# Full-row dummies and tap broadcast, and filter block 1 transposed beside the rows of y, in a fused SSM and GEGLU kernel

## The chip, the cores and the metric

The kernel runs on one core of a Trainium2 chip. The metric is the device time of one execution in microseconds (us), taken as the median of several runs. A core has five engines with a queue of instructions each: TensorE (PE, matmuls, its weight loads shown as PEld), VectorE (DVE), ScalarE (ACT), GpSimd (POOL) and SyncE (SP, which here only issues DMAs). They wait for each other through semaphores. Matmuls write to PSUM; the kernel uses PSUM as four slots of two banks, a slot being 128 partitions of 2 x 512 32-bit words.

## The reference, cut to what matters

Four sublayers act on x of 2048 positions and 576 channels (bf16): an SSM convolution, a gated feed-forward of width 4608, and both once more.

```python
def _A_ref(q, k, v, shift_k, ssm_k, ssm_D):
    for t in range(ks):                       # ks = 4
        k_shift = k_shift + k_pad[:, t:t + S, :] * shift_k[:, ks - 1 - t][None, None, :]
    kv = k_shift * v
    kv_f, kf_f = rfft(pad(kv)), rfft(pad(ssm_k))
    y = irfft(kv_f * kf_f)[:S] + kv * ssm_D
    return q * y
def _B_ref(x, w_gate, w_up, w_down):
    return (_gelu(x @ w_gate) * (x @ w_up)) @ w_down
x = A_q
x = x + _A_ref(_layernorm(x), A_k, A_v, A_shift_k, A_ssm_k, A_ssm_D)
x = x + _B_ref(_layernorm(x), B_w_gate, B_w_up, B_w_down)
...
```

The last two lines are applied a second time with the same weights.

## The kernel before

The 2048 positions are cut into four blocks of 512, and a block into four rows of 128 partitions (row j holds positions 4p + j). The convolution is done by block with transforms of length 512 written as matmuls, so each block of `kv` and of the filter `ssm_k` is transformed by matmuls with a matrix T of sines, multiplied on VectorE and transformed back with V, the transpose of T. The feed-forward of a block runs over 36 tiles of 128 hidden columns in three passes: gate and up matmuls (`gu`, L1008), Gelu on ScalarE, the product on VectorE, then down matmuls (`dn`, L1576). The convolutions of later blocks are woven into these matmuls.

The opening, up to the first gate/up matmuls of block 0, is laid out by a planner (`Plan`): each piece of work is a task with an engine, a cost, tasks it depends on, a priority, and sometimes a PSUM slot (`bank=True`) that comes free when all tasks naming it in `frees` have run. The planner puts the tasks in an order by these costs, and each engine's queue is written in that order. What the steps of the change touch there, in order of time:

- `ones` (L1101, L1110) is a tile of one row, and 16 dummy matmuls (L1137) use it for both operands while the first loads come in.
- `sk1` (L1099) holds the four taps of the shift filter in one row. `tap` (L1187) broadcasts each tap over 128 partitions by a matmul with `ones` (L1191), and ScalarE copies it to `skc` (L1193).
- VectorE multiplies the block's `k` by the taps (L1209), TensorE sums these products in PSUM with an identity or a shifted identity (L1218), and VectorE multiplies the sums by `v` (L1229).
- `turned_h` (L1238) transposes a block of the filter, loaded as `hn`, with TensorE (L1251): two groups of ten transposes, each with a PSUM slot of its own, each copied out by ScalarE for block 0 and by VectorE for block 1 (L1253). Block 1's come last, with the lowest priority; they are next read by the filter's transform woven into the feed-forward (L290).
- Filter block 0 and `kv` block 0 are transformed (L281, L275), multiplied (L316 to L320) and transformed back to y (L1340): rows 0 and 2 as soon as the products come, rows 1 and 3 after them. The four rows of y take the four PSUM slots. A row of y uses 288 of the 512 columns of each bank.
- `busy` (L1366): ten times four dummy matmuls with the identity, into spare columns of the slot of row 1 of y.
- For each row j, in the order 0, 2, 1, 3 of the source: `factor` (L1385, ScalarE, reads y and makes `yh`), `gate` (L1394, VectorE, makes the new x and its sum), `nm` and `nu` (L1399, L1401: the negative mean, twice, scaled in two ways), the copy of y out of PSUM (L1404, ScalarE), `square` (L1411, ScalarE), `root` (L1419, L1420, GpSimd), `norm` (L1427, VectorE, makes `xn`), ten transposes of `xn` (L1439, L1441, TensorE) into a PSUM slot, and the copy to `xnT` (L1446 by VectorE, L1449 by ScalarE).
- `gu_half`: the first two gate/up tiles start with half of the columns, those of rows 0 and 2, as soon as these two are there.

In the order that the planner made, row 2 comes first, then 0, 3 and 1.

Of the kernel before, what the change touches and what calls it, by code (L numbers as in the profile page):

```python
# [10 lines left out]
ACT = mybir.ActivationFunctionType  # L11
# [682 lines left out]
def ssm_geglu_kernel(ctx, tc, A_q, A_k, A_v, A_shift_k, A_ssm_k, A_ssm_D, B_x, B_w_gate, B_w_up,  # L694
# [394 lines left out]
    with tc.manual_schedule():  # L1089
# [6 lines left out]
        with ExitStack() as es:  # L1096
            tmp = es.enter_context(tc.tile_pool(name="s_tmp", bufs=1))
            hp = es.enter_context(tc.tile_pool(name="s_h", bufs=1))
            sk1 = tmp.tile([1, D, conv.KS], BF16, name="sk1")  # L1099
            drow = tmp.tile([1, D], BF16, name="drow")  # L1100
            ones = tmp.tile([1, P], BF16, name="ones")  # L1101

            def load_hn(b):
# [5 lines left out]
                return hn  # L1109
            nc.vector.memset(ones[:], 1.0)  # L1110
            below = tmp.tile([P, P], BF16, name="below")
            for grid in (ident, below):
                nc.gpsimd.memset(grid[:], 0.0)
            nc.sync.dma_start(out=sk1[:].rearrange("p d j -> p (d j)"),
                              in_=A_shift_k.rearrange("d j -> (d j)").unsqueeze(0))
# [19 lines left out]
            ps = bank(3, "ps")  # L1135
            for _ in range(16):
                nc.tensor.matmul(ps[:, 0, 0:P], lhsT=ones[:], rhs=ones[:], start=True, stop=True)  # L1137
# [46 lines left out]
            vneg = add("ACT", 0.9, vnegs, [vsin], prio=-20.0)  # L1184


            def tap(j):  # L1187
                def fill_ps(task):
                    ps = psum(("tap", j), task)
                    for h in range(2):  # L1190
                        nc.tensor.matmul(ps[:, h, 0:HW], lhsT=ones[:], rhs=sk1[:, h * HW:(h + 1) * HW, j], start=True, stop=True)  # L1191
                a = later(lambda me: add("PE", 0.5, me(fill_ps), bank=True, ready=2.9))
                return add("ACT", 0.65, lambda: nc.scalar.copy(out=conv.halves(conv.skc[:, j, :]),  # L1193
                                                               in_=held.pop(("tap", j))[:, :, 0:HW]), [a], lat=0.1, frees=[a])
# [42 lines left out]

            def turned_h(b, dep, ready, prio):  # L1238
                outs = []
                for g in range(RT // 2):  # L1240
                    def fill_ps(task, g=g):
                        if b == 0 and g == 0:
                            hT[0] = lambda i: hT0[:, i, :]
                        elif b == 1:
                            pairs1.append(conv.hrp.tile([P, 2, D], BF16, tag="hr", name="ht"))
                            hT[1] = conv.ht[1] = lambda i: pairs1[i // 2][:, i % 2, :]
                        pt = psum(("h", b, g), task, (P, 2, 1024), BF16)
                        for i in range(2):
                            for db in range(ND):
                                w = min(P, D - db * P)  # L1250
                                nc.tensor.transpose(pt[:, i, db * P:db * P + w], hn[b][0:w, db, 2 * g + i:BS:RT], ident[0:w, 0:w])  # L1251
                    a = later(lambda me: add("PE", 1.05, me(fill_ps), dep, bank=True, ready=ready, prio=prio))
                    outs.append(add("DVE" if b else "ACT", 0.8 if b else 1.12, lambda g=g: (nc.vector.tensor_copy if b else nc.scalar.copy)(out=hT0[:, 2 * g:2 * g + 2, :] if b == 0 else pairs1[g][:], in_=held.pop(("h", b, g))[:, :, 0:D]),  # L1253
                                    [a], lat=0.1, frees=[a], prio=prio))
                return outs

            h0 = {}

            def filter_tile(m, deps):
# [12 lines left out]
                return outs  # L1272
            t0 = turned_h(0, [], HN_AT, 30.0)
            for a in opens:
# [89 lines left out]
            def busy():  # L1364
                for _ in range(4):
                    nc.tensor.matmul(held["y", 1][:, 1, 384:512], lhsT=ident[:], rhs=ident[:], start=True, stop=True)  # L1366
            chain([add("PE", 0.22, busy, [inv[1], inv[3]], frees=[opened[1]], prio=-100.0) for _ in range(10)])


# [11 lines left out]
            for j in (0, 2, 1, 3):  # L1381

                def factor(j=j):
                    held["yh", j] = tmp.tile([P, 2, HW], F32, tag="yh", bufs=2, name="yh")
                    nc.scalar.activation(out=held["yh", j][:], in_=held["y", j][:, :, 0:HW], func=ACT.Identity,  # L1385
                                         scale=g0[j]["rstd"][:, 0:1], bias=1.0)
                fa = add("ACT", 0.65, factor, [inv[j], stat[j]] + pluses[-2:-1], lat=0.1)

                def gate(j=j):
# [8 lines left out]
                    v["nm"] = small.tile([P, 1], F32, tag="l_nm", name="nm")  # L1398
                    nc.vector.tensor_single_scalar(out=v["nm"][:], in_=v["s"][:], scalar=-1.0 / D ** 1.5, op=ALU.mult)  # L1399
                    v["nu"] = small.tile([P, 1], F32, tag="nu", name="nu")  # L1400
                    nc.vector.tensor_single_scalar(out=v["nu"][:], in_=v["s"][:], scalar=-1.0 / D, op=ALU.mult)  # L1401
                gp = add("DVE", 1.1, gate, [fa])
                pluses.append(gp)
                copies[j] = add("ACT", 0.65, lambda j=j: nc.scalar.copy(out=conv.halves(conv.y[0][:, j, :]), in_=held.pop(("y", j))[:, :, 0:HW]),  # L1404
                    [fa], frees=[opened[j]], prio=-10.0)

                def square(j=j):
                    v = vs0[j]
                    v["ss"] = small.tile([P, 1], F32, tag="ss", name="ss")
                    junk = work.tile([P, D], BF16, tag="ga", name="junk")  # L1410
                    nc.scalar.activation(out=junk[:], in_=x_c[0][:, j, :], func=ACT.Square, bias=v["nm"][:, 0:1],  # L1411
                                         scale=1.0 / math.sqrt(D), accum_out=v["ss"][:])
                sq = add("ACT", 0.96, square, [gp], lat=0.1)

                def root(j=j):
                    v = vs0[j]
                    v["rstd"] = small.tile([P, 1], F32, tag="l_rstd", name="rstd")
                    ve = small.tile([P, 1], F32, tag="ve", name="ve")
                    nc.gpsimd.tensor_scalar(out=ve[:], in0=v["ss"][:], scalar1=EPS, scalar2=None, op0=ALU.add)  # L1419
                    nc.gpsimd.tensor_tensor(out=v["rstd"][:], in0=ve[:], in1=neghalf_t[:, 0:1], op=ALU.pow)  # L1420
                rt = add("POOL", 0.85, root, [sq], lat=0.05)

                def norm(j=j):
                    v = vs0[j]
                    xn, entry = xn_tile()
                    held["xn", j], entry[0] = xn, True
                    nc.vector.tensor_scalar(out=xn[:, 0:D], in0=x_c[0][:, j, :], scalar1=v["nu"][:, 0:1],  # L1427
                                            scalar2=v["rstd"][:, 0:1], op0=ALU.add, op1=ALU.mult)
                no = add("DVE", 0.6, norm, [rt])

                def turn_xn(task, j=j):
# [3 lines left out]
                    for b in range(NKC):  # L1435
# [5 lines left out]
                        nc.tensor.transpose(pt[:, b // 8, (b % 8) * P:(b % 8 + 1) * P], held["xn", j][:, c0:c0 + P], ident[:])  # L1441
                tx = later(lambda me: add("PE", 0.55, me(turn_xn), [no], bank=True))
                tok = slice(j * P, (j + 1) * P)
# [10 lines left out]

            t1 = turned_h(1, [loads[1]] + [pA[part, m, 0] for part in range(2) for m in (0, 2)] + H0[3] + K0[3], 0.0, -30.0)
            conv.nhr = 6
# [218 lines left out]
```

## Time and profile before

| what | us |
|---|---|
| median of three runs | 929.02 (928.86 to 929.34) |
| the profiled run's own time | 928.66 |
| its span in the profile | 926.9 |
| TensorE busy | 917.0 |
| first dummy matmul | 1.06 |
| filter block 0 transposed from | 6.61 |
| y transformed back from, to | 31.04, 36.92 |
| first transposes of xn | 41.02 |
| first half gate/up matmul | 44.03 |

The profile is of one execution. A line of the timeline gives the start and the length of a group of like instructions (the length reaches to the end of the last one, which overlaps with what follows), engine, line, operation, the tiles written and read, shape and type, and how many; in square brackets stands the time for which the engine had been idle, and what it was waiting for. The share of the span is written in tenths or per cent; the granted clock of TensorE is a number from 0 to 1.

### The profile page before, as it was taken

To read this page: it belongs to the slowest core of one execution; us is meant where nothing else is said; L and a number is where in the kernel's file an instruction comes from. 1 tells how busy PE (TensorE), PEld (TensorE's weight loads), DVE (VectorE), ACT (ScalarE), POOL (GpSimd) and SP (SyncE) were. 2 spreads that over 40 slices of the span, in tenths; PEclk is the share of its full clock that TensorE was granted. 3 is DMA by queue.
4 is the path that set the end of the run, shared out by engine and by line. 5 is a ranking of instruction groups with operands and counts; after the bars stand their busy time and mean duration, and the time that the engine had idled before them with its cause. 6 is when DMAs were issued, how large, how long until landed. Compare 5 with 4: busy or idle time off the path is not lost.

```text
span 926.9 us, 19167 instructions
## 1 busy us (share of the span) xinstructions
PE 917.0 (99%) x8103; PEld 529.8 (57%) x8103; DVE 579.7 (63%) x1109; ACT 325.7 (35%) x594; POOL 139.9 (15%) x305
## 2 busy tenths in 40 slices
PE   9999999999999999999999999999999999999998
PEld 6746456564664655646646646546556556556555
DVE  7876876777898898768988873553332334433332
ACT  6664525643215136252122223451221224321211
POOL 3314102312014002230112101220000002100000
PEclk9999999999999999999999999999999999999999
DMA  9899997337726901991952820690820730797620
GB/s 238 267 236 239 265 254 139 117 77 218 205 65 153 251 2 21 218 281 36 240 166 76 168 78 27 124 196 15 152 80 1 145 87 14 132 214 162 144 68 27
DMA packets 125307, 129.69 MB, mean 140 GB/s; under 512 B 39714, under 2 KB 117411, under 8 KB 125220
## 3 DMA queue, kind: packets, MB, share of 16 engines
q1 hardware_dynamic: 116018, 92.92, 46.9%
q0 software_dynamic: 9056, 34.95, 11.7%
q8 instruction: 63, 1.03, 0.5%
q10 hardware_dynamic: 146, 0.59, 0.2%
q14 instruction: 24, 0.20, 0.1%
HBM read 108.09 MB, written 11.80 MB: 129 GB/s over the span
## 4 chain that ended last, share of the span: by engine, by line
PE 95%; DVE 2%; ACT 1%; issue 0%; DMA 0%; POOL 0%; ACTq 0%; DVEq 0%; SPq 0%
PE gu L1008 60%; PE dn L1576 28%; PE ps L281 1%; PE cps L290 1%; PE cps L343 1%; PE ps L1218 1%; DVE kc L602 1%; PE cps L301 0%; PE ps L1008 0%; PE ps L1340 0%; PE ps L1251 0%; DVE ab L308 0%; DVE cd L308 0%; ACT eo L303 0%; DMA xnT<-xn 0%
## 5 line engine op out<-in xcount | busy, mean ns | idle before, releaser
L1008 PE MATMUL gu<-xnT,wgu 64*128 64x512 bf16 x5148 | 561.1, 376 | 2.3 <-DVE x_c L1618 1.5
L1008 PEld LDWEIGHTS <-wgu 64*128 64x128 bf16 x5220 | 255.2, 94 | 304.3 <-issue 9.9
L1557 ACT ACTIVATE ga<-gu 128x512 f32<-128x512 f32 x256 | 152.8, 597 | 471.4 <-PE gu L1008 465.3
L1558 DVE TENSOR_TENSOR hT<-ga,gu 128x512 bf16<-128x512 f32 x256 | 175.5, 685 | 204.3 <-ACT ga L1557 203.0
L1576 PE MATMUL dn<-wd,hT 128*128 128x288 bf16 x2304 | 294.1, 286 | 0.0
L1576 PEld LDWEIGHTS <-hT 128*128 128x128 bf16 x2304 | 223.5, 98 | 65.3 <-issue 9.3
L840 POOL TENSOR_SCALAR means<-s 128x1 f32<-128x1 f32 x28 | 11.8, 421 | 237.7 <-DVE x_c L1612 205.3
L1620 DVE TENSOR_TENSOR x_c<-x_c,dn 128x576 f32<-128x576 f32 x32 | 24.1, 752 | 31.0 <-PE dn L1576 30.9
L1618 DVE SCALAR_TENSOR_TENSOR x_c<-dn,means,x_c 128x576 f32<-128x576 f32 x28 | 22.7, 815 | 26.8 <-PE dn L1576 26.7
L856 POOL TENSOR_TENSOR rstd<-ve,neghalf_t 128x1 f32<-128x1 f32 x56 | 35.5, 635 | 4.7
L320 DVE TENSOR_TENSOR prod<-prod 128x576 bf16<-128x576 bf16 x72 | 33.0, 458 | 2.5
L1547 ACT ACTIVATE ga<-gu 128x512 bf16<-128x512 f32 x30 | 17.9, 597 | 44.1 <-PE gu L1008 42.1
L303 ACT ACTIVATE eo<-cps 128x576 f32<-128x576 f32 x32 | 20.4, 650 | 25.0 <-DVE ab L308 9.8
L418 POOL DMA_DIRECT2D kr<-Kd x24 | 13.2, 550 | 87.1 <-DVE prod L319 86.1
L1599 DVE TENSOR_TENSOR xn<-x_c,dn 128x576 bf16<-128x576 f32 x15 | 11.3, 752 | 24.0 <-PE dn L1576 23.9
L422 POOL DMA_DIRECT2D hr<-Hd x36 | 19.4, 540 | 41.2 <-DVE prod L319 38.5
L602 DVE TENSOR_TENSOR kc<-ab,cd 128x288 bf16<-128x288 f32 x64 | 25.6, 450 | 0.0
L1549 DVE TENSOR_TENSOR hT<-ga 128x512 bf16<-128x512 bf16 x31 | 13.1, 421 | 18.5 <-ACT ga L1548 18.5
L840 POOL TENSOR_SCALAR nm<-s 128x1 f32<-128x1 f32 x28 | 8.7, 312 | 99.9 <-DVE x_c L892 99.8
L848 ACT ACTIVATE junk<-x_c,nm 128x576 bf16<-128x576 f32 x28 | 21.5, 767 | 4.9 <-POOL nm L840 4.9
L882 ACT ACTIVATE yh<-y,rstd 128x576 f32<-128x576 bf16 x28 | 21.4, 768 | 2.3 <-POOL rstd L856 2.3
L855 POOL TENSOR_SCALAR ve<-ss 128x1 f32<-128x1 f32 x56 | 15.3, 273 | 42.9 <-ACT junk L848 42.8
(170 smaller groups left out, 607.1 us busy)
## 6 DMA issues: line engine op xcount, KB each, us to landing
wgu<-in_B_w_gate_dram SPq DMA_DIRECT2D x45, 576.0 KB, 6.2
wd<-in_B_w_down_dram SPq DMA_DIRECT2D x30, 864.0 KB, 8.0
wgu<-in_B_w_up_dram SPq DMA_DIRECT2D x45, 512.0 KB, 8.3
hr<-Hd POOLq DMA_DIRECT2D x36, 288.0 KB, 7.9
kr<-Kd POOLq DMA_DIRECT2D x24, 288.0 KB, 6.7
Kd<-kc POOLq DMA_DIRECT2D x12, 288.0 KB, 6.3
k<-in_A_k_dram POOLq DMA_DIRECT2D x3, 1008.0 KB, 11.1
wgu<-in_B_w_up_dram SPq DMA_DIRECT2D x45, 64.0 KB, 8.7
```

The source lines that it names most:

```text
L320: nc.vector.tensor_tensor(out=dst[:, cols], in0=pr[:, 0, cols], in1=pr[:, 1, cols], op=ALU.subtract if part == 0 else ALU.add)
L602: nc.vector.tensor_tensor(out=into[k][:, plane, cols], in0=a, in1=b, op=op)
L840: nc.gpsimd.tensor_scalar(out=v["nm"][:], in0=v["s"][:], scalar1=-1.0 / D, scalar2=None, op0=ALU.mult)
L848: nc.scalar.activation(out=junk[:], in_=get_x(), func=ACT.Square, bias=v["nm"][:, 0:1], accum_out=v["ss"][:])
L856: nc.gpsimd.tensor_tensor(out=v["rstd"][:], in0=ve[:], in1=neghalf_t[:, 0:1], op=ALU.pow)
L882: nc.scalar.activation(out=g["yh"][:], in_=conv.y[c][:, j, :], func=ACT.Identity, scale=g["rstd"][:, 0:1], bias=1.0)
L1008: nc.tensor.matmul(cols(pair[:, s, :]), lhsT=w[r0:r0 + HK, k, gi * P:(gi + 1) * P], rhs=cols(xnT[r0:r0 + HK, blk_of[k], :]), start=(k == 0 ...
L1557: nc.scalar.activation(out=ga[:], in_=pair[:, 0, :], func=ACT.Gelu_apprx_tanh)
L1558: nc.vector.tensor_tensor(out=hT[:, fi, :], in0=ga[:], in1=pair[:, 1, :], op=ALU.mult)
L1576: nc.tensor.matmul(acc[:, h, 0:HW], lhsT=hT[:, fi, j * P:(j + 1) * P], rhs=wd[2 * wb + fi // WT][:, fi % WT, h * HW:(h + 1) * HW], start=( ...
L1618: nc.vector.scalar_tensor_tensor(out=xh, in0=acc[:, :, 0:HW], scalar=m_[:, 0:1], in1=xh, op0=op, op1=ALU.add)
L1620: nc.vector.tensor_tensor(out=xh, in0=xh, in1=acc[:, :, 0:HW], op=ALU.add)
```

## The change

1. `ones` gets 128 rows, and the dummies are 18 instead of 16. `sk1` gets 97 rows: the taps are loaded to the last one, the others are set to zero by VectorE, and the tap broadcast multiplies 97 rows. After the last tap two more dummies (`spare`) write to spare columns of its slot.
2. `turned_h` is split. Block 0's stays as it was. Block 1's (`turned_h1`) takes no PSUM slot: of its two groups the columns from 128 on go into unused columns of the slots of rows 1 and 3 of y, seen as bf16, and the first 128 columns of both groups into the slot of row 0. Four copies by VectorE (two of 2 x 128 columns, two of 2 x 448) take the place of two of 1152 columns. The slots of rows 0, 1 and 3 come free only after these copies too.
3. `busy` is 8 times 4 dummies of 96 columns instead of 10 times 4 of 128, in the slot of row 0.
4. Priorities: the factor of row 1, the squares and roots of rows 0 and 2, and the copies of y. `nu` goes; `nm` takes its scale, and the square and the root are scaled to suit.

In the order of the changed program TensorE has all twenty transposes of block 1 right behind y's rows, then the dummies, and none between the gate/up matmuls. On ScalarE the order of kinds is unchanged; of the last three copies of y, row 3 now comes before 0, and row 1 last. On VectorE the first strip copy stands before the gate of row 1, the copy out of row 3's slot after it and before the norm of row 2, the second strip after the norm of row 3, and the copy out of row 1's slot between the two copies to `xnT`. The queues of GpSimd and SyncE keep their order.

```diff
-            sk1 = tmp.tile([1, D, conv.KS], BF16, name="sk1")
+            SK = 3 * P // 4
+            sk1 = tmp.tile([SK + 1, D, conv.KS], BF16, name="sk1")
-            ones = tmp.tile([1, P], BF16, name="ones")
+            ones = tmp.tile([P, P], BF16, name="ones")
...
+            nc.vector.memset(sk1[0:SK, :, :], 0.0)
...
-            nc.sync.dma_start(out=sk1[:].rearrange("p d j -> p (d j)"),
+            nc.sync.dma_start(out=sk1[SK:SK + 1, :, :].rearrange("p d j -> p (d j)"),
...
-            for _ in range(16):
+            for _ in range(18):
                 nc.tensor.matmul(ps[:, 0, 0:P], lhsT=ones[:], rhs=ones[:], start=True, stop=True)
...
+            def spare(ps):
+                for _ in range(2):
+                    nc.tensor.matmul(ps[:, 1, 3 * P:4 * P], lhsT=ones[:], rhs=ones[:], start=True, stop=True)
...
-                        nc.tensor.matmul(ps[:, h, 0:HW], lhsT=ones[:], rhs=sk1[:, h * HW:(h + 1) * HW, j], start=True, stop=True)
+                        nc.tensor.matmul(ps[:, h, 0:HW], lhsT=ones[0:SK + 1, :], rhs=sk1[:, h * HW:(h + 1) * HW, j], start=True, stop=True)
+                    if j == 0:
+                        spare(ps)
...
+            def turned_h1(dep):
+                W = D - P
+                beside = lambda j: held["y", j].bitcast(BF16)
+                hT[1] = conv.ht[1] = lambda i: pairs1[i // 2][:, i % 2, :]
+                for g, j in ((0, 1), (1, 3)):
+                    def fill_ps(g=g, j=j):
+                        pairs1.append(conv.hrp.tile([P, 2, D], BF16, tag="hr", name="ht"))
+                        for i in range(2):
+                            for db in range(ND):
+                                w = min(P, D - db * P)
+                                out = beside(j)[:, i, 2 * HW + (db - 1) * P:2 * HW + (db - 1) * P + w] if db else \
+                                    beside(0)[:, g, 2 * HW + i * P:2 * HW + (i + 1) * P]
+                                nc.tensor.transpose(out, hn[1][0:w, db, 2 * g + i:BS:RT], ident[0:w, 0:w])
+                    a = add("PE", 1.05, fill_ps, dep + [opened[0], opened[1], opened[3]], prio=-30.0)
+                    add("DVE", 0.2, lambda g=g: nc.vector.tensor_copy(
+                        out=pairs1[g][:, :, 0:P], in_=beside(0)[:, g, 2 * HW:2 * HW + 2 * P].rearrange("p (i d) -> p i d", i=2)),
+                        [a], frees=[opened[0]], prio=-10.0 if g else 10.0)
+                    add("DVE", 0.6, lambda g=g, j=j: nc.vector.tensor_copy(
+                        out=pairs1[g][:, :, P:D], in_=beside(j)[:, :, 2 * HW:2 * HW + W]), [a], frees=[opened[j]], prio=3.0 if g else -30.0)
...
-                    nc.tensor.matmul(held["y", 1][:, 1, 384:512], lhsT=ident[:], rhs=ident[:], start=True, stop=True)
-            chain([add("PE", 0.22, busy, [inv[1], inv[3]], frees=[opened[1]], prio=-100.0) for _ in range(10)])
+                    nc.tensor.matmul(held["y", 0][:, 1, 416:512], lhsT=ident[:], rhs=ident[:, 0:96], start=True, stop=True)
+            chain([add("PE", 0.22, busy, [inv[1], inv[3], opened[0]], frees=[opened[0]], prio=-100.0) for _ in range(8)])
...
-                fa = add("ACT", 0.65, factor, [inv[j], stat[j]] + pluses[-2:-1], lat=0.1)
+                fa = add("ACT", 0.65, factor, [inv[j], stat[j]] + pluses[-2:-1], lat=0.1, prio=15.0 if j == 1 else 0.0)
...
-                    nc.vector.tensor_single_scalar(out=v["nm"][:], in_=v["s"][:], scalar=-1.0 / D ** 1.5, op=ALU.mult)
-                    v["nu"] = small.tile([P, 1], F32, tag="nu", name="nu")
-                    nc.vector.tensor_single_scalar(out=v["nu"][:], in_=v["s"][:], scalar=-1.0 / D, op=ALU.mult)
+                    nc.vector.tensor_single_scalar(out=v["nm"][:], in_=v["s"][:], scalar=-1.0 / D, op=ALU.mult)
...
-                    [fa], frees=[opened[j]], prio=-10.0)
+                    [fa], frees=[opened[j]], prio=-50.0 if j == 1 else -30.0 if j == 0 else -10.0)
...
-                nc.gpsimd.tensor_scalar(out=ve[:], in0=v["ss"][:], scalar1=EPS, scalar2=None, op0=ALU.add)
+                nc.gpsimd.tensor_scalar(out=ve[:], in0=v["ss"][:], scalar1=1.0 / D, scalar2=EPS, op0=ALU.mult, op1=ALU.add)
...
-            t1 = turned_h(1, [loads[1]] + [pA[part, m, 0] for part in range(2) for m in (0, 2)] + H0[3] + K0[3], 0.0, -30.0)
+            turned_h1([loads[1], inv[1], inv[3]])
```

## The prediction

> **What bounds the kernel now.** I read the page first: engines, then the chain of work that ended last.
>
> ```profile
> PE 917.0 (99%) x8103; PEld 529.8 (57%) x8103; DVE 579.7 (63%) x1109; ACT 325.7 (35%) x594; POOL 139.9 (15%) x305
> ...
> PE 95%; DVE 2%; ACT 1%; issue 0%; DMA 0%; POOL 0%; ACTq 0%; DVEq 0%; SPq 0%
> ```
>
> TensorE is busy for 99% of the span. So time can be won in two ways only: PE works faster, or PE is given less to do. The edits all lie before the first gate/up matmuls, so next I read the timeline of PE over the first 50 us.
>
> ```profile
> 1.06 1.88 PE L1137 MATMUL ps<-ones 1*128 1x128 bf16 x16 [1.06 <-DVE pis L1132]
> 3.00 2.20 PE L1191 MATMUL ps<-sk,ones 1*128 1x288 bf16 x8
> 5.48 1.12 PE L1218 MATMUL ps<-kvt,below 128*128 128x288 bf16 x4 [0.28 <-ACT skc L1193]
> 6.61 2.95 PE L1251 MATMUL ps<-ident,hn 128*128 128x128 bf16 x20
> 9.49 1.62 PE L1218 MATMUL ps<-kvt,below 128*128 128x288 bf16 x6
> 10.91 1.32 PE L1218 MATMUL ps<-kvt,ident 128*128 128x288 bf16 x6
> 12.06 0.61 PE L1180 MATMUL ps<-ident,T 128*128 128x128 bf16 x8
> ...
> 13.73 1.88 PE L1218 MATMUL ps<-kvt,ident 128*128 128x288 bf16 x14
> ...
> 36.92 1.04 PE L1251 MATMUL ps<-ident,hn 128*128 128x128 bf16 x10
> 38.13 2.39 PE L1366 MATMUL ps<-ident 128*128 128x128 bf16 x40 [0.18 <-ACT yh L1385]
> 41.02 0.38 PE L1441 MATMUL ps<-ident,xn 128*128 128x128 bf16 x4 [0.49 <-ACT y L1404]
> ...
> 44.03 2.14 PE L1008 MATMUL ps<-xnT,wgu 64*128 64x256 bf16 x36
> 46.10 1.07 PE L1251 MATMUL ps<-ident,hn 128*128 128x128 bf16 x10
> 46.95 1.19 PE L1008 MATMUL ps<-xnT,wgu 64*128 64x256 bf16 x18
> ```
>
> Two things are to be seen. First, the same 128x288 matmul starts every 0.24 us from 9.49 (six in 1.42 us) but every 0.123 us from 13.73 (14 until 15.45); the six from 10.91 take 1.15 us, so the change of rate falls among them, near 11.7 (three at 0.24, then 0.12). PE runs at half rate until then, though the granted clock reads 1.00 in every window. Second, from 5.48 to 30.3 PE is never idle; it is idle again at 30.3 to 31.0, 38.0 to 38.1 and 40.5 to 41.0. At 46.10, with PE in demand, ten transposes of filter block 1 stand on the path: 46.10 to 46.95.
>
> **Head: full-row dummies and taps.** In the old kernel the dummies (L1137) and the tap broadcast (L1191) use one row of the array. They kept PE going from 1.06 to 5.2 at half rate (16 dummies, 0.107 us each) and did not raise it: the first full-row work begins at 5.48, the rate rises near 11.7. The new dummies use 128 rows, the taps 97 (96 of zeros). Two dummies more (0.21 us) fit the wait before 3.00, two spare ones after the last tap the 0.28 us before 5.48: nothing.
>
> If full-row work counts from 1.06, the rate rises 11.7 - 5.48 = 6.2 us after it or sooner, that is by 7.3. The Trainium skill (TensorE: Matmul & The Clock Gate, Part 1: The HAM clock gate) says that PE starts at half clock and is released after one busy window of about 3.4 us that runs freely, not from the kernel's start. By that alone the old kernel would be fast by 7.9 at the latest; the trace says 11.7, so here one-row work did not count; for the new one an estimate from the page is 4.5 to 7.9.
>
> Worth at full rate: the first four matmuls (5.48) end early but the transposes still wait until 6.61 for `hn` (the view of that tile shows 0.7 us of PE waiting for its two transfers). Twenty transposes took 2.88 us (6.61 to 9.49); at full rate ten take 0.85 (46.10 to 46.95) to 1.04 (36.92), so 0.96 each and 0.12 for the second piece of `hn`: 2.04, a gain of 0.84. Twelve accumulating matmuls took 2.57 (9.49 to 12.06), at 0.123 they take 1.47: gain 1.10. Sum 1.94. If the rate rises at 7.3, five transposes go at the old 0.144 instead of 0.096: 0.24 less. I take 1.9.
>
> Can the others follow? VectorE's fourth product ends at 4.53 + 4 x 0.68 = 7.3, before its matmuls; the product with `v` (L1229) then starts at 10.1 instead of 12.02. By the view of DMA issues `v` lands 6.2 us after its issue at 2.23, so at 8.4, and `x_b` for the statistics 7.1 after 2.85, at 9.95, before they are wanted at 12.7. ScalarE's first copy of the transposes moves from 8.15 to 7.85, the second from 9.59 to 8.95; the table load (1.28), `V` copy and negations behind it move 0.7 to 1.2, and it had 0.74 us idle at 16.63; it just keeps up. From 17.4 to 30.4 PE is contiguous, so the gain stays.
> The new memset of 96x1152 words on VectorE has no row; the memset of 128 columns took 0.17, which scales to 1.5 at most, and the smallest took 0.06. I take 1.2, nearer the first. It moves the angle steps from 1.91 to about 2.2 and the products by 0.1 to 0.4; the cover is the wait for `hn`. Without it, 0.4 would be lost.
>
> **Tail: filter block 1.** In the old kernel its second ten transposes run at 46.10, because the first ten hold a bank from 36.92 to the copy at 41.63 and no further bank is free. Now all twenty follow y in unused columns of its banks 0, 1 and 3, and the ten at 46.10 go: from the last half gate/up matmul (44.03 + 36 x 0.0545 = 45.99) to 46.95 is 0.96, and the wait of the next filter matmuls (48.08) for their copy (47.20 + 0.76) goes too, 0.1. Gain 1.06 at most.
>
> What it pushes, in times of the old trace (all minus the head's gain): twenty transposes 36.92 to 38.85. The factor of row 1 (L1385, the second of two at 36.71, begun at 37.35) reads a bank just written, so it stands behind the first ten: 38.05, 0.7 late. Behind it on ScalarE wait the squares, on VectorE the gate of row 1. The old dummies in spare columns of row 1's bank, which began only on "ACT yh L1385", show that waits go by bank, not by column.
>
> ```profile
> 36.71 1.37 ACT L1385 ACTIVATE yh<-ps,rstd 128x576 f32<-128x576 f32 x2
> 37.97 0.77 ACT L1411 ACTIVATE junk<-x_c,nm 128x576 bf16<-128x576 f32 x1
> ...
> 40.35 1.16 ACT L1404 CAST y<-ps 128x576 bf16<-128x576 f32 x2
> 41.94 1.12 ACT L1449 COPY xnT<-ps 128x1152 bf16<-128x1152 bf16 x1 [0.44 <-PE ps L1441]
> ```
>
> - ScalarE: squares at 38.67, 39.43 and 40.27, copies of y 3 and y 0 at 41.05 and 41.57 to 42.2, then xnT at 42.1.
> - VectorE: gate 3 to 38.45; a strip of 256 columns, which needs the sixteenth transpose (38.6); by the 1152-column copy of 0.75 it takes 0.2 (0.06 to 0.75 bound it); gate 1 38.9 to 39.9; 896 columns 0.6, to 40.45; xn of row 2 40.45 to 41.0 (old: 39.46), row 0 to 41.5, row 3 to 42.1, the second strip after y 0's copy to 42.5, row 1 to 43.1. Four times 0.07 for `nu` is saved.
> - PE: the four rows take 0.73 each from 41.05, 41.78, 42.51, 43.25 and end at 44.0; the old ones began at 41.02, held by "ACT y L1404", and ended at 44.03.
>
> So the bank's wait goes, VectorE takes its place, and the half matmuls start as before. The tight spot is the second strip (42.5 against 42.51): late by up to 0.5 if both new copies cost their 0.75, on time otherwise. Tail: 1.06 less 0.5 at worst, gain 0.95 taken. The smaller dummy block (32 x 96 columns for 40 x 128) lies in PE's wait from 39.0 to 41.0: nothing, unless the clock falls (below). From there the orders of all engines are the old ones but for a few products of VectorE that swap places and one pair of down matmuls; PE is the bound, and its waits at 159 to 168, 194 to 198 and 229 to 244 hang on chains that move with it: nothing, give or take 0.3.
>
> **Sum.** 1.9 + 0.95 = 2.85 off the profiled run's 928.66 (span 926.9 and 1.8 around it) gives 925.8. The median shown, 929.02, lies 0.36 above that run, which would give 926.2. I forecast 926.0.
>
> **Rivals.**
> - *The clock rises no sooner* (the edit does not do what it says): zeros and ones for operands, or work this early, do not count. For it: work at 1.06 to 5.2 counted for nothing once. Against: all that differed was its rows. The head then gives 0, the tail 0.95: 929.02 - 0.95 = 928.1.
> - *The tail gives its gain back.* The factor's 0.7 and the new copies go through ScalarE and VectorE to the fourth xn instead of into PE's old wait of 0.49. For it: the second strip has no slack. Only the head is left: 929.02 - 1.9 = 927.1.
> - *Slower: the clock falls before the gate/up matmuls.* Now twenty transposes follow y, then a dummy block shorter by a third (32 x 96 against 40 x 128 columns), then forty transposes. If transposes do not count as work, the clock falls near 41. Against: in the old trace 40.3 to 44.0 had nothing but transposes and a pause and stayed fast (44.03, 36 half matmuls in 2.07). Price: the forty transposes take 2.9 us and would take half as long again (0.144 against 0.096 in the head), 1.5 more, and half rate for the 6.2 us of the head from 44.0 on, 3.1; with both gains kept 929.02 - 2.85 + 4.6 = 930.8. It decides once half rate lasts over 2.7 us into the matmuls (2.85 - 1.5 = 1.35 lost, twice that long).
> The Trainium skill (TensorE: Matmul & The Clock Gate, Part 4: PE-mode transpose) says that transposes do not count as PE-busy in the same way and that the full clock does not engage for them; in this trace transposes from 36.92 on go at full rate, so I give the rival little.
>
> **Chances and range.** Forecast 0.62, clock no sooner 0.15, tail gives back 0.12, slower 0.07, nothing at all 0.04. Measurement tells a change from none beyond 0.2%, 1.86 us, that is below 927.16. Faster: 0.60 of the forecast and 0.07 of the tail's rival, 0.67; slower: part of the slow rival and mishaps, 0.06; same 0.27. Range: both gains at their ends (1.94 + 1.06) and 0.3 of later waits from the lower run, with as much again for spread, 928.66 - 3.3 - 0.4 = 924.9; upward to the clock's rival with 0.5 for spread, 928.6.
>
> **What would show it.** Right: 128x288 matmuls 0.123 apart from 9.5 at the latest; the second transposes' end near 8.7; y's inverse 1.9 earlier; transposes in one run of twenty, none between half gate/up matmuls; xn transposes contiguous. Wrong: 0.24 spacing past 9.5 (head), a wait of PE on VectorE over 0.3 between the rows' transposes (tail), 0.144 per transpose near 41 (slow rival).

## The result, and the profile after

| | us | runs |
|---|---|---|
| before, median | 928.88 (928.23 to 929.61) | 17 |
| after, median | 926.01 (925.33 to 928.82) | 17 |
| ratio after / before | 0.9973 [0.9967, 0.998] | |
| profiled run before, span | 928.66, 926.9 | 1 |
| profiled run after, span | 925.93, 924.2 | 1 |

The forecast was 926.0, and the kernel is faster by 0.27%; the interval of the ratio does not reach 1. One thing was not foreseen: the 17 times fall into two groups, 13 from 925.33 to 926.99 and four from 928.00 to 928.82, with nothing between. The experiments show what the second group is; below, its executions are called late, by their time alone (927.7 or more in a kernel that has the whole tail); where a trace of one exists, it is shown. The profiled run belongs to the first group.

The page of the kernel after, engines and then the shares of the chain by engine:

```profile
PE 914.6 (99%) x8099; PEld 529.2 (57%) x8099; DVE 580.8 (63%) x1108; ACT 325.5 (35%) x594; POOL 140.9 (15%) x305
...
PE 96%; DVE 3%; ACT 1%; issue 0%; DMA 0%; POOL 0%; ACTq 0%; DVEq 0%; SPq 0%
```

TensorE still bounds the kernel. It is busy for 2.4 us less (917.0 to 914.6) and the span is 2.7 us shorter. The timeline of PE in the kernel after (start, length, line, tiles, count, idle time before and its end):

```profile
1.08 2.10 PE L1139 MATMUL ps<-ones 128*128 128x128 bf16 x18 [1.08 <-DVE ones L1111]
3.24 2.20 PE L1197 MATMUL ps<-sk,ones 97*128 97x288 bf16 x8
5.26 0.39 PE L1190 MATMUL ps<-ones 128*128 128x128 bf16 x2
5.72 1.12 PE L1226 MATMUL ps<-kvt,below 128*128 128x288 bf16 x4
6.63 2.27 PE L1255 MATMUL ps<-ident,hn 128*128 128x128 bf16 x20
8.83 0.91 PE L1226 MATMUL ps<-kvt,below 128*128 128x288 bf16 x6
9.58 0.90 PE L1226 MATMUL ps<-kvt,ident 128*128 128x288 bf16 x6
10.31 0.61 PE L1182 MATMUL ps<-ident,T 128*128 128x128 bf16 x8
...
35.17 2.04 PE L1275 MATMUL ps<-ident,hn 128*128 128x128 bf16 x20
37.27 1.52 PE L1392 MATMUL ps<-ident 128*128 128x96 bf16 x32
39.24 0.40 PE L1466 MATMUL ps<-ident,xn 128*128 128x128 bf16 x4 [0.44 <-DVE xn L1452]
...
42.29 3.12 PE L1008 MATMUL ps<-xnT,wgu 64*128 64x256 bf16 x54
45.35 0.66 PE L290 MATMUL cps<-ht,T 128*128 128x288 bf16 x4
```

The last of these in the kernel before:

```profile
48.08 0.67 PE L290 MATMUL cps<-ht,T 128*128 128x288 bf16 x4
```

All twelve accumulating matmuls now run at the full rate (8.83 to 10.31, 0.123 each). Set beside the old timeline, the difference can be read at four places: the transposes for `V` start at 10.31 for 12.06 (1.75 earlier), the inverse of y ends at 35.17 for 36.92 (1.75), the first half gate/up matmul starts at 42.29 for 44.03 (1.74), and the filter matmuls behind the half matmuls start at 45.35 for 48.08 (2.73). So the head gave 1.75, nothing was lost on the way, the tail gave 0.99, and the sum of 2.7 is still there at the end of the span. In the tail the twenty transposes of filter block 1 are one run behind y, and 54 half matmuls follow one another with no transposes among them.

The same stretch on VectorE and ScalarE in the kernel after:

```profile
36.93 0.29 DVE L1277 COPY ht<-ps 128x256 bf16<-128x256 bf16 x1 [0.18 <-PE ps L1275]
37.14 0.81 DVE L1420 SCALAR_TENSOR_TENSOR x_c<-x_b,mv,yh 128x576 f32<-128x576 bf16 x1
...
38.07 0.63 DVE L1280 COPY ht<-ps 128x896 bf16<-128x896 bf16 x1
38.61 1.72 DVE L1452 TENSOR_SCALAR xn<-x_c,nm,rstd 128x576 bf16<-128x576 f32 x3
40.40 0.29 DVE L1277 COPY ht<-ps 128x256 bf16<-128x256 bf16 x1
...
36.30 0.74 ACT L1411 ACTIVATE yh<-ps,rstd 128x576 f32<-128x576 f32 x1 [0.59 <-PE ps L1275]
```

ScalarE's factor of row 1 waits for the ten transposes that write in its bank. On VectorE the gate (L1420), a strip of 896 columns and three rows of xn follow one another; PE's first transposes of xn wait for "DVE xn L1452".

### The profile page after: what moved, and what is told of

The parts are those of the page before. It is cut to its first block, busy times and chain, and to the rows that moved or that the text cites. A ratio compares the mean times of both kernels' runs of the same rounds, so it can differ in the third digit from the quotient of the medians.

```text
span 924.2 us, 19158 instructions
## 1 busy us (share of the span) xinstructions
PE 914.6 (99%) x8099; PEld 529.2 (57%) x8099; DVE 580.8 (63%) x1108; ACT 325.5 (35%) x594; POOL 140.9 (15%) x305
## 4 chain that ended last, share of the span: by engine, by line
PE 96%; DVE 3%; ACT 1%; issue 0%; DMA 0%; POOL 0%; ACTq 0%; DVEq 0%; SPq 0%
PE gu L1008 60%; PE dn L1601 28%; PE ps L281 1%; PE cps L290 1%; PE cps L343 1%; PE ps L1366 1%; DVE kc L602 1%; PE ps L1226 1%; PE cps L301 0%; PE ps L1008 0%; DVE ab L308 0%; DVE cd L308 0%; ACT eo L303 0%; DMA xnT<-xn 0%; PE ps L1466 0%
## 5 line engine op out<-in xcount | busy, mean ns | idle before, releaser
L1572 ACT ACTIVATE ga<-gu 128x512 bf16<-128x512 f32 x30 | 17.9, 597 | 44.0 <-PE gu L1008 42.1
L422 POOL DMA_DIRECT2D hr<-Hd x36 | 19.4, 540 | 41.2 <-DVE prod L319 39.1
```

## The experiments

Twelve runs of eleven kernels (s5_again is s5_spare once more), in three sets; each ratio is against the kernel before on the same chip. The diffs of the first two leave out one half of the change; the others are against the changed kernel.

**The two halves alone.** h1_head is the kernel before with the new `ones`, `sk1`, memset, 18 dummies and spares; t1_tail is the changed kernel with these lines as they were.

```diff
 h1_head, against the kernel before:
-            sk1 = tmp.tile([1, D, conv.KS], BF16, name="sk1")
+            sk1 = tmp.tile([SK + 1, D, conv.KS], BF16, name="sk1")
-            ones = tmp.tile([1, P], BF16, name="ones")
+            ones = tmp.tile([P, P], BF16, name="ones")
+            nc.vector.memset(sk1[0:SK, :, :], 0.0)
-            for _ in range(16):
+            for _ in range(18):
...
+                    if j == 0:
+                        spare(ps)
 t1_tail, against the kernel after: the same lines the other way round
```

> The head alone: 128-row dummies, 97-row taps, spares and the memset, with the old tail (block 1's second ten transposes between the gate/up matmuls). Theory A (two gains that add): y's last matmul 1.75 us earlier than before (35.17 against 36.92), so 1.75 faster, 927.1, in most executions; the ten transposes at 46.1 stay. Rival B (the head's gain is only passed on to a wait later in the opening): under 0.5 us. In some executions, one in four, the rate may rise as late as before: then no gain, so two groups of times about 2 us apart.

> The tail alone: one-row dummies and taps as before, transposes of filter block 1 behind y and the new priorities. Theory A: the start of the first half gate/up matmul stays at 44.0, the matmuls behind the second half start 1.0 us earlier; 0.95 to 1.0 faster, 927.9, and one group of times only. Rival B (the tail gives its gain back through the late factor of row 1): under 0.4 us.

The head alone: 926.94 median (926.30 to 929.54), ratio 0.9982 [0.9973, 0.9991]; nine of its eleven times lie from 926.30 to 927.57 and two at 929.29 and 929.54. The tail alone: 927.74, ratio 0.9986 [0.9977, 0.9995]. Each half is worth something by itself, and 0.18% and 0.14% agree within their intervals with the 0.27% of both.

In the profile of t1_tail it is 10.17 us from the transposes of filter block 1 (37.95) to the filter matmuls (48.12), as in the kernel after (10.18, 35.17 to 45.35) and 0.99 less than before (36.92 to 48.08): the tail's gain does not hang on the head. The times of t1_tail are not the one narrow group that was expected: they spread over 2.4 us, and its profiled run (928.72) suggests why: the rate rises at 13.87, where the same old head in the profiled run before had it at 11.76. So the 1.75 of the head is the difference of two executions, and not a mean.

The profiled run of h1_head was one of the two late ones. Its timeline of PE:

```profile
3.24 2.20 PE L1198 MATMUL ps<-sk,ones 97*128 97x288 bf16 x8
5.26 0.39 PE L1191 MATMUL ps<-ones 128*128 128x128 bf16 x2
5.77 1.12 PE L1227 MATMUL ps<-kvt,below 128*128 128x288 bf16 x4
6.68 2.96 PE L1260 MATMUL ps<-ident,hn 128*128 128x128 bf16 x20
9.57 1.62 PE L1227 MATMUL ps<-kvt,below 128*128 128x288 bf16 x6
10.99 1.65 PE L1227 MATMUL ps<-kvt,ident 128*128 128x288 bf16 x6
12.43 0.88 PE L1182 MATMUL ps<-ident,T 128*128 128x128 bf16 x8
```

The same instructions start at the same times as in the kernel after up to 5.3, and yet all twelve accumulating matmuls run at half rate (six take 1.42 from 9.57) and the rate rises only among the transposes for `V`, near 13.0. So this late execution is one in which the new head did not raise the rate early.

The traces hold one more thing, the throttle's own records. The lengths between two changes of the rate that they give (914.77, 918.18, 880.64, 34.13 and 6.83 us in several kernels) are whole multiples of 3.413 us: 268, 269, 258, 10 and 2. Changes come on a grid of 3.413 us, and the grid lies differently in each execution: first rises were at 7.12 (after), 11.76 (before) and 12.98 (the late h1_head). The times of the profiled runs that have the new tail go with the rise: 925.66 to 926.38 where it came at 4.48 to 7.12 (s5_again, s6_filled, x1_strip_twice, s5_spare, after), and 927.89, 928.23, 928.57 and 928.72 where it came at 12.14, 12.85, 13.54 and 13.87 (k12_gaps, p2_one_row_dummies, p1_one_row_taps, t1_tail). In these last four, a rise that comes 1.73 us later costs 0.83, about half of it. The Trainium skill (TensorE: Matmul & The Clock Gate, Part 1: The HAM clock gate) speaks of a free-running window of 3413 ns; the traces agree.

That gave a theory: the rate rises at the end of the first stretch of the grid in which PE paused for little. There are two pauses left in the new head, between the dummies and the taps (the last dummy starts at 2.87 and takes 0.107, the first tap starts at 3.24: 0.26) and between the spares and the first accumulating matmuls (5.45 to 5.72: 0.27). A stretch that holds both would fail. In the late h1_head that is 2.74 to 6.15. The next stretch, 6.15 to 9.57, failed too, though the timeline shows no idle time of PE in it: nearly all of it (6.68 to 9.57) is the twenty transposes, five in 0.72 us where five steps of 0.107 would take 0.54 at most. Read from their starts, about 1.0 us of this stretch lies between the matmuls. That these small gaps made it fail fits the grid, and no run varies them.

**Filling the pauses.** s5_spare (and s5_again) has more spares, s6_filled also more dummies:

```diff
 s5_spare, s5_again:
-                for _ in range(2):
+                for _ in range(5):
 s6_filled: spares range(4), and
-            for _ in range(18):
+            for _ in range(20):
```

> The changed kernel with five spare dummies instead of two after the last tap: they fill PE's wait before 5.72 (0.28 us). Of 17 runs of the changed kernel 13 took 925.3 to 927.0 and 4 took 928.0 to 928.8. Theory P (the rate rises at the end of a stretch of some 3.4 us that was full enough of full-row matmuls, and where such a stretch begins differs from run to run; transposes do not fill it): 0.3 us more matmul work lifts the poorest stretch, so fewer or no runs near 928.3, the others unchanged near 925.8. Rival Q (the slow group has to do with landing transfers or with something later): the same share, one in four, stays near 928.3.

> The changed kernel with 20 dummies in place of 18 and four spare matmuls in place of two: the pauses of PE near 3.0 and 5.5 us shrink to less than 0.1 us each. Theory (pauses decide which executions are late): no late executions, all within 925.4 to 926.7, median 925.9, where the changed kernel had 4 late of 17. Rival (late executions come from elsewhere): about one in four is near 928.2 again.

> The changed kernel with five spare matmuls in place of two (the second pause near 5.5 us filled), once more for a larger number of executions. Theory: again no late execution, all within 925.4 to 926.7, median 925.9. Rival (the five runs of the first time missed the late ones by chance): about a quarter near 928.2.

s5_spare: 925.89 (925.58 to 926.38), ratio 0.9967 [0.9955, 0.998]. s6_filled: 926.17 (925.66 to 926.74), 0.9968 [0.9956, 0.9981]. s5_again: 925.65 (925.55 to 926.19), 0.9966 [0.9953, 0.9978]. Together 15 executions and not one late, ten of them with five spares. With the two spares of the change, ten of 28 were late (four of 17 of the kernel after and six of eleven of x1_strip_twice below, which has the same head); at that rate ten in a row without one would have a chance of (18/28)^10, 1.2%, and of 7% at the rate of the kernel after alone. The head of s5_again, and below it the transposes in s5_spare:

```profile
5.26 0.46 PE L1190 MATMUL ps<-ones 128*128 128x128 bf16 x5
5.72 0.65 PE L1226 MATMUL ps<-kvt,below 128*128 128x288 bf16 x4
6.57 2.07 PE L1255 MATMUL ps<-ident,hn 128*128 128x128 bf16 x20 [0.20 <-DMA hn<-in_A_ssm_k_dram]
```

```profile
7.63 1.72 PE L1255 MATMUL ps<-ident,hn 64*128 64x64 bf16 x16 [0.62 <-DMA hn<-in_A_ssm_k_dram]
```

The fifth spare starts at 5.50, and the accumulating matmuls begin at 5.72 as before (at 5.76 in s5_spare, where the rate was still low), so the spares cost next to nothing and little is left of the second pause. Within the early group the landing of `hn` still sets the head: s5_spare waits 0.62 for it and starts the transposes for `V` 0.72 later than s5_again (10.77 for 10.05), which is what its profiled run is longer by (926.38 for 925.66). In s6_filled the edit missed half of its aim: with 20 dummies the taps simply begin later, at 3.54, behind a pause of 0.35 that no dummy fills, and the spares leave 0.2. Its five runs are no test of the first pause. s5 is the version to take: the ten executions of the two s5 runs have a mean of 925.82 where the kernel after has 926.45. Its median (925.74 for 926.01) and its ratio are not told apart from those of the kernel after; what it removes is the late executions.

**Making the pauses wider.** k12_gaps:

```diff
-            for _ in range(18):
+            for _ in range(12):
...
-                    if j == 0:
-                        spare(ps)
```

> The changed kernel with 12 dummies in place of 18 and without the two spare matmuls: PE is idle from about 2.35 to 3.24 us (0.9) and from 5.26 to 5.72 (0.46). Theory (the rate is raised at the end of a 3.41 us stretch with less than about half a microsecond of idle PE; the stretches lie differently in each execution): only stretches that begin behind 3.2 us can pass early, so most executions are late ones, near 928, and the median rises from 926.0 to 927.5 to 928.2. Rival (the sum of full-row work since the start counts, 0.9 us of it is gone): the rise comes about 0.9 us later, half of it matters: median 926.5.

927.94 (926.85 to 929.11), ratio 0.9991 [0.9982, 1.0]: the number of the theory, and nearly the whole gain of the head gone. The place of the pause was wrong, as its timeline shows:

```profile
1.08 1.46 PE L1139 MATMUL ps<-ones 128*128 128x128 bf16 x12 [1.08 <-DVE ones L1111]
2.60 2.20 PE L1197 MATMUL ps<-sk,ones 97*128 97x288 bf16 x8
5.68 1.12 PE L1224 MATMUL ps<-kvt,below 128*128 128x288 bf16 x4 [0.88 <-ACT skc L1199]
```

The taps did not stay at 3.24 but followed the shorter dummies, so the wide pause (0.88) lies behind them. The taps were never waiting for a transfer: the first starts 0.37 behind the start of the last dummy with 12 (2.23 to 2.60) as with 18 (2.87 to 3.24), and 0.46 behind it with 20 (3.08 to 3.54, s6_filled).

**Which rows matter.** p2_one_row_dummies was meant to put dummies and spares back on one row, with the taps left on 97; p1_one_row_taps does the reverse.

```diff
 p2_one_row_dummies (dummies):
-                nc.tensor.matmul(ps[:, 0, 0:P], lhsT=ones[:], rhs=ones[:], start=True, stop=True)
+                nc.tensor.matmul(ps[:, 0, 0:P], lhsT=ones[0:1, :], rhs=ones[0:1, :], start=True, stop=True)
 p1_one_row_taps (sk1 with one row, no memset of it):
-                        nc.tensor.matmul(ps[:, h, 0:HW], lhsT=ones[0:SK + 1, :], ...
+                        nc.tensor.matmul(ps[:, h, 0:HW], lhsT=ones[0:1, :], ...
```

> The changed kernel with its 18 dummies and two spare matmuls back on one row, the taps left on 97 rows. Theory (one-row work counts as a pause, and 3.41 us nearly without pauses are needed): full-row work starts at 3.2 us instead of 1.1, and only a stretch that begins between about 2.9 and 3.7 us can pass early, so most executions rise near 10 to 13 us: median 927.6 to 928.1. Rival (the taps' 2.1 us of 97-row work were the missing part): 926.0 to 926.3, the same as with the changed kernel.

> The changed kernel with the taps back on one row (and without the memset of 96 rows), the 18 dummies and two spares left on 128 rows. Theory: the taps' 2.1 us are a pause in the middle of every stretch that could pass early, so almost no execution rises before 9 us: median 927.6 to 928.2, like the tail alone. Rival (the dummies' 1.9 us of full rows are enough, the taps only lose the time of the memset): 926.0 or a little below.

In p2_one_row_dummies the spares stayed on 128 rows; the edit reached the dummies alone. It measured 926.48 (925.80 to 928.54), ratio 0.9979 [0.997, 0.9987]: six executions from 925.80 to 926.48 and five late. That is neither the theory's 927.6 to 928.1 nor clearly worse than the kernel after: six early of eleven against 18 of 28 can't be told apart. The theory left room for about a quarter of early executions (stretches that begin between 2.9 and 3.7, 0.8 of 3.41 us), so six of eleven speak against one-row dummies being no more than a pause. p1_one_row_taps: 928.51 (927.73 to 928.90), ratio 0.9995 [0.9987, 1.0004]; all eleven are late, and the head has no gain left. So the taps' rows are needed, in the middle of the stretches that matter; that the dummies' rows help is not shown.

**Does one row count at all, and do transposes?** d2_one and d3_turn put 64 dummies of a kind in a row, long enough (6.8 us) to hold at least one whole stretch of the grid.

```diff
-            for _ in range(18):
+            for _ in range(64):
...
 d2_one:
+                nc.tensor.matmul(ps[:, 0, 0:P], lhsT=ones[0:1, :], rhs=ones[0:1, :], start=True, stop=True)
 d3_turn (ps in bf16):
+                nc.tensor.transpose(ps[:, 0, 0:P], ones[:], ident[:])
```

> The changed kernel with 64 dummies in place of 18, and these on one row of the array (1x128 by 1x128) in place of 128. They run without a pause for 64 x 0.107 = 6.8 us at half rate, so the taps and all that follows start some 5 us late and the time (about 930) is not the point. Theory (the rate rises at the end of a stretch of 3.41 us in which the array had full-row work nearly throughout; one row does not count): all 64 start 0.107 us apart, and the rate rises only after the taps (97 rows) and the matmuls behind them. Rival (what counts is that PE is kept going, whatever the rows, and the old head failed for its pauses only): two whole stretches of 3.41 us lie in the 64, so the distance falls from 0.107 to 0.055 among them, and they end some 1.5 us sooner.

> The changed kernel with 64 dummies in place of 18, each a full-row 128x128 transpose of the ones against the identity; they begin when the identity is built, near 2.2 us, and run without a pause. Theory (transposes count as work): the distance between their starts falls from 0.107 to about 0.055 within 3.4 to 6.9 us of their start, so among the 64. Rival (the skill's rule that transposes do not count as busy): all 64 start 0.107 us apart, for 6.8 us, and the rate rises only behind the matmuls that follow. The time (930 or so) is not the point.

The 64 one-row matmuls of d2_one, in the timeline of PE, and the accumulating ones behind them:

```profile
1.08 7.00 PE L1139 MATMUL ps<-ones 1*128 1x128 bf16 x64 [1.08 <-DVE ones L1111]
8.14 2.20 PE L1197 MATMUL ps<-sk,ones 97*128 97x288 bf16 x8
...
15.84 1.65 PE L1226 MATMUL ps<-kvt,ident 128*128 128x288 bf16 x6
```

At 15.84 six accumulating matmuls still go at the half rate: the one-row work did not raise it, and the rise came at 17.9. The dummies' line by form, first for d2_one and then for d3_turn (shortest, median and longest duration of one in ns, then first and last start):

```profile
L1139 PE MATMUL ps<-ones x64: 284/309/309, 1.1 to 7.8; 1*128 1x128 bf16 x64
```

```profile
L1139 PE MATMUL ps<-ident,ones x64: 219/314/314, 2.2 to 8.4; 128*128 128x128 bf16 x64
```

In d2_one the 64 start over 6.7 us, 63 steps of 0.107. In d3_turn they start over 6.2 and the shortest is 219 ns: the last ones go at the full rate, from the throttle's record at 7.99 on, with nothing but transposes since 2.2. The Trainium skill (TensorE: Matmul & The Clock Gate, Part 4: PE-mode transpose) says that transposes do not count as busy in the same way and that the full clock does not engage for them; this trace shows otherwise on both. The times (933.21 and 930.71 in one run each) only reflect the longer head.

**The slow rival.** n1_nobusy leaves out the dummy block behind filter block 1:

```diff
-            chain([add("PE", 0.22, busy, ..., prio=-100.0) for _ in range(8)])
+            chain([add("PE", 0.22, busy, ..., prio=-100.0) for _ in range(0)])
```

> The changed kernel without the 32 dummies between block 1's transposes and those of xn (they leave no result that is used). Theory: the dummies keep the rate up; without them PE has from 35.2 to 42.3 only transposes and a pause of some 2 us. If transposes do not count as work, the rate falls near 39 to 42, the transposes of xn or the half gate/up matmuls run at half rate, and the time rises by 1.5 to 4.6 us (927.5 to 930.6). Rival: transposes count, or the pause is too short to matter: no change, 926.0.

927.45 (926.86 to 929.55), ratio 0.9988 [0.9979, 0.9996], 1.4 us above the median after and just below the 927.5 to 930.6 of the theory; none of the eleven is under 926.86. Only one has a trace, so how the rate went in the others, and how many were late in the head, is not known. PE in front of the transposes of xn, and then windows of its profiled run (928.77), all engines, the clock third from the end:

```profile
39.48 0.61 PE L1466 MATMUL ps<-ident,xn 128*128 128x128 bf16 x4 [2.03 <-DVE xn L1452]
```

```profile
36.00:38.00 2.00, 1.45 (x15) 1.00 (x14) 1.80 (x5) 1.46 (x4) 0.13 (x1) 1.00 0.51 190
38.00:40.00 2.00, 0.52 (x4) 0.34 (x4) 1.89 (x7) 2.00 (x7) 1.70 (x5) 0.77 0.42 79
40.00:42.00 2.00, 2.00 (x19) 1.55 (x19) 1.35 (x3) 1.70 (x3) 0.55 (x1) 0.50 0.99 290
42.00:44.00 2.00, 2.00 (x19) 1.37 (x18) 1.29 (x2) 0.69 (x2) 0.00 (x0) 0.50 1.04 222
44.00:46.00 2.00, 2.00 (x20) 1.38 (x22) 0.76 (x1) 1.00 (x2) 0.00 (x0) 0.52 0.34 112
46.00:48.00 2.00, 2.00 (x42) 1.74 (x38) 0.00 (x0) 0.00 (x0) 0.00 (x0) 1.00 0.95 248
```

PE waits 2.03 us for the first xn; the clock falls at 39.1 and is back two stretches of the grid later, at 45.9. The forty transposes of xn take 4.97 us (39.48 to 44.45) where the kernel after needs 3.05, and the 54 half matmuls 3.82 for 3.12: 2.6 us, which with 0.25 of a later head is the 2.84 by which this run is longer than the profiled run after. What the rival feared, a fall of the clock before the gate/up matmuls, is real in this execution; with the 32 dummies the clock of the profiled run after stays at 1.00.

**Is VectorE the gate of the tail?** x1_strip_twice makes the 896-column copy at 38.07 twice:

```diff
-                    add("DVE", 0.6, lambda g=g, j=j: nc.vector.tensor_copy(
-                        out=pairs1[g][:, :, P:D], in_=beside(j)[:, :, 2 * HW:2 * HW + W]), [a], ...
+                    def rest(g=g, j=j):
+                        for _ in range(1 + g):
+                            nc.vector.tensor_copy(out=pairs1[g][:, :, P:D], in_=beside(j)[:, :, 2 * HW:2 * HW + W])
+                    add("DVE", 0.6, rest, [a], ...
```

> The changed kernel with VectorE's first 896-column copy of filter block 1 (at 38.07 us, 0.63) made twice, the same data to the same place. Theory (VectorE has taken the old bank's place as what the transposes of xn wait for, as predicted): row 2's transposes start 0.55 later against the end of y's inverse (4.07 us behind its start of transposes in the changed kernel, then 4.6), the four rows and the first half gate/up matmul follow by as much, and the time rises by 0.55 to about 926.6. Rival (they still wait for a bank or for ScalarE, VectorE has slack): the first half gate/up matmul stays 7.1 us behind the start of the hn transposes, and the time stays at 926.0.

The timeline of PE, then of VectorE:

```profile
34.70 2.02 PE L1275 MATMUL ps<-ident,hn 128*128 128x128 bf16 x20
36.79 1.52 PE L1394 MATMUL ps<-ident 128*128 128x96 bf16 x32
39.41 0.40 PE L1468 MATMUL ps<-ident,xn 128*128 128x128 bf16 x4 [1.10 <-DVE xn L1454]
...
42.44 3.12 PE L1008 MATMUL ps<-xnT,wgu 64*128 64x256 bf16 x54
```

```profile
37.59 1.28 DVE L1282 COPY ht<-ps 128x896 bf16<-128x896 bf16 x2
38.79 1.55 DVE L1454 TENSOR_SCALAR xn<-x_c,nm,rstd 128x576 bf16<-128x576 f32 x3
```

From the transposes of filter block 1 to those of xn it is 4.71 us (34.70 to 39.41) for 4.07, and to the first half gate/up matmul 7.74 for 7.12: the 0.65 of the second copy goes to PE in full. So VectorE has no slack there (shown at the place of this copy). The median, 928.84 (926.04 to 929.33, ratio 0.9988 [0.9979, 0.9998]), says nothing on it, since six of eleven executions were late in the head; the five early ones have a median of 926.41, 0.6 above the 925.81 of the 13 early ones of the kernel after.

## Why the prediction was right

- *What bounds the kernel, and the sum.* Right: 2.85 was forecast off the profiled run, 2.73 came off. The head measured 1.75 for 1.9, the tail 0.99 for 0.95. (The lower end of the range comes to 924.96 by its own terms, not 924.9.)
- *Luck, in part.* The median hit 926.0 because only four of the 17 executions were late. In x1_strip_twice, with the same head, six of eleven were; at such a share the median here would have been about 928. The two groups were not foreseen. The head's size was also taken off one execution, and the old head's rise moves (11.76 before, 13.87 in t1_tail).
- *The size of the head.* The twenty transposes take 2.20 (6.63 to 8.83), a gain of 0.68 for 0.84, since the rate rose at 7.12, after the first few of them; that is the case costed at 0.24 less. The twelve accumulating matmuls take 1.48 for the forecast 1.47.
- *Why the rate rises.* One-row work alone does not raise it: right (d2_one, p1_one_row_taps), though one-row dummies in front of full-row taps did not harm as much as a pause would (p2_one_row_dummies). That full-row work from 1.06 on counts from its start was too simple: the taps' rows decide, and the rise comes at a grid point behind a stretch with little pause. "The rate rises ... by 7.3" therefore holds, judged by their times, for 18 of 28 executions; in the late one with a trace, h1_head, it fails by 5.7 us. The forecast time was that of the early ones.
- *Costed at nothing: two dummies and two spares.* "Fit the wait before 3.00" was wrong: there is no wait, the taps moved from 3.00 to 3.24 and the first accumulating matmuls from 5.48 to 5.72. It cost nothing because the old wait for `hn` (6.39 to 6.61 by the starts) covered it: the transposes begin at 6.63 for 6.61. The spares left a pause of 0.27, and filling it took the late executions away in s5_spare and s5_again; that a pause could decide it was not seen.
- *The memset.* Bounded from 0.06 to 1.5, taken as 1.2; it took 1.02, and the angle steps began at 2.15, the first product at 4.70. Covered, as forecast.
- *The tail.* Shifted by the head's 1.75, the steps came as written: the factor of row 1 at 38.05 (36.30 + 1.75; forecast 38.05), the transposes of xn from 40.99 (forecast 41.05), the first half gate/up matmul at 44.04 (old 44.03). The bank's wait went, and VectorE took its place (x1_strip_twice). The copies came near their sizes, 896 columns 0.63 for 0.6 and 256 columns 0.29 for 0.2. The second strip, at 42.15 and only 256 columns (0.29), was in time.
- *Rivals.* "The clock rises no sooner" is what a late execution is, some third of them: its 928.1 lies within the late group, 928.00 to 928.82. "The tail gives its gain back" is out (0.99 kept). The slow one does not occur in this kernel; without the dummies its clock fell, at 39.1 instead of 41. The price there was 2.6 us, not 4.6, since half rate lasted 6.8 us and not beyond. The stretch that made it fall (35.68 to 39.09) held transposes and a pause; as transposes alone raised the rate in d3_turn, the pause is the likelier cause, but n1_nobusy does not separate the two.
- *The clock's row.* "The granted clock reads 1.00 in every window" while PE ran at half rate: the prediction was right to go by the starts. The row is no measurement before the first change of the rate: in d2_one all 64 dummies run at half rate under a 1.00, while behind the first record it is right (0.50 in n1_nobusy from 40 to 44). The distance between like instructions told the rate.

## What to carry to other kernels

To bring TensorE to its full rate early, fill its idle opening with work on many rows and leave no pause in it: look at the pauses between groups, not only at the first start, and fill them where a filler costs nothing, until the executions no longer fall into two groups. When a median hides two groups, read each by itself, or a change of 0.6 us can look like one of 2.8. Before costing an instruction at nothing because it fits a wait, see in the trace who ends that wait; here the next group simply followed the last dummy.

## What was not expected of the hardware

- Changes of the rate come on a grid of 3.413 us whose phase differs from execution to execution. A stretch with pauses of 0.26 and 0.32 us (2.74 to 6.15 in the late h1_head) did not pass; one with a single pause of 0.35 (1.86 to 5.27 in s6_filled) did, and one with 0.26 and 0.12 (2.15 to 5.57 in x1_strip_twice). Counted by the starts, with the small gaps between transposes, the fullest stretches that passed held 0.51 (8.34 to 11.76 in the kernel before) and 0.56 us (42.51 to 45.92 in n1_nobusy), the emptiest that failed without one-row work 0.58 (the late h1_head). A limit near half a microsecond fits these, but they lie too close together to measure it, and gaps between transposes need not weigh as much as waits.
- One-row matmuls alone did not raise the rate (64 in a row, 6.7 us, in one execution); 97 rows count (p1_one_row_taps without them, none early), and 128-row transposes too (d3_turn, one execution: rise after 5.8 us of nothing else).
- After a pause of 1.6 us within a stretch (37.45 to 39.09 in n1_nobusy, transposes before it) the rate fell; with one of 1.1 (38.31 to 39.41 in x1_strip_twice) it did not.
- What stays open: whether full rows in the dummies help (p2_one_row_dummies: five late of eleven, against ten of 28), the exact limit of the pause, whether the gaps between transposes count like waits, and what a pause alone does to a rate that is up.
